# Weight decode without a clamp, scales from column sums, and plain f32 scores for the first eight jobs

## The chip, the core and the metric

The kernel runs on one core of a Trainium2 chip. The metric is the device time of one execution in microseconds. Five engines work beside each other, each taking its own queue of instructions in order: PE (TensorE, matrix products into PSUM), DVE (VectorE), ACT (ScalarE), POOL (GpSimd) and SP, which issues most transfers. Transfers run on 16 DMA engines. Semaphores order the engines; an instruction at the head of a queue that waits holds everything behind it.

## The reference

Attention over 8 batches x 8 heads, 576 positions, 64 numbers a head, then a two-layer network with an odd activation:

```python
scores = scale * np.matmul(q, k.transpose(0, 1, 3, 2))       # scale = 1/8
cum = np.cumsum(np.maximum(s, 0.0), axis=-1)
bias = -(cum[:, :, :, None] - cum[:, :, None, :])
scores = np.where(causal, -1000000000.0, scores + np.minimum(bias, 0.0))
attn = softmax(scores)                                        # sum + 1e-9
x = (attn @ v) as (4608, 512)
h = x @ w_in                                                  # (512, 2048)
g = np.where(h >= 1, h, np.where(h <= -1, 0.0, (h + 1) ** 2 / 4.0))
out = (g @ w_out).astype(np.float32)                          # (2048, 512)
```

q, k, v and s come as float32, the two weights as float64: each weight is read as two 32-bit words.

## The kernel before, in words

**Attention.** A job is a pair of heads and a half of the query positions (320 or 256 of them): 64 jobs, 8 to a batch, jobs 0 to 3 the first halves of batch 0 and jobs 4 to 7 its second halves. `att_load` brings q and k of the job into the raw tiles rq and rk, each twice, into partitions 0 to 63 and 64 to 127. `att_prep` makes from them two pairs of tiles in a reduced f32 form (float32r): Q1 and K1 hold the rounded values (and in the upper half what rounding left of q), Q2 and K2 what rounding left of k, against the rounded q, and four rows more that carry the running sum of s in two parts (`cum`), so that the bias comes out of the same product. It takes three ACT operations (L325, L334, L335), one of DVE (L336) and one of DVE or POOL (L339; POOL for jobs 0 to 11), and two small transfers on ACT's queue for the cum rows. `scores` multiplies Q1 by K1 (L384) and adds Q2 by K2 (L385) in PSUM, six units a job; DVE adds the mask and takes the minimum (L390), ACT the exponent (L401), `weights_t` normalises and splits the weights into two float16 parts (L417 to L428) and a transposing transfer turns them (pt<-pb). `att_out` multiplies with v (L447) and writes the job's piece of the tile x (L458, L459).

**Network.** A half of a batch is one unit. `ffn_h` makes 16 hidden tiles (12 products each, L502), each turned into u by ACT (L514) and DVE (L517, L518) and split into two float16 parts g (L528, L529); `ffn_y` multiplies with the second weight (L541). Three products stand for each product of a float16 pair.

**Weights.** `Weights.decode` turns a tile of 128 x 512 float64 numbers into float32 bits, `scale` finds a power of two from the largest value of a group of tiles, `split` makes the float16 pair. Each weight has 16 tiles. The first weight (w1, tiles wir, held in WO, result WI) is one group; the second (w2, tiles wor, result WO) two groups. In `scale` the maxima of 128 partitions go through PE twice: a transpose (L107) and a product with ones that spreads the result (L117).

**Order.** The program writes the first four jobs with w1's decode in between, then w1's scale and splits, then the loop in which attention runs ahead of the network and w2 is decoded within the first hidden tiles. A scheduler of the language, which works with its own estimate of time and with priorities, then sets the order on each engine's queue. `load(c + 3)` keeps three raw weight tiles ahead of the decode.

## Time and profile before

| | us |
|---|---|
| runs: median, lowest, highest of 3 | 1128.73, 1127.24, 1128.74 |
| profiled execution, span from first to last instruction | 1126.2 |
| profiled execution, own time | not listed apart from its span |
| PE busy | 988.1 (88% of the span) |
| weight loads of PE, beside it | 771.8 (69%) |
| DVE busy | 876.6 (78%) |
| ACT busy | 745.2 (66%) |
| POOL busy | 693.1 (62%) |
| read from HBM, written | 75.33 MB, 9.73 MB |

A row of a group reads: line, engine, operation, out<-in, shapes, count | busy us, mean ns of one | idle us before them and what ended it. A row of the timeline reads: start us, duration us, engine, line. A row of waits reads: who waited for whom: us in total, times, longest. A row by stretches has for PE, its weight loads, DVE, ACT and POOL the busy time and the instructions in brackets, then the clock granted to PE as a share of full speed, the DMA engines' share and their rate in GB/s.

### The profile page before, as it was taken

The page shows a single profiled execution, that of the slowest core. Times are in us where ns is not written, and L with a number is a line of the kernel's source. Part 1 is how long each engine was busy: PE and PEld are TensorE (multiplying, and loading weights), DVE is VectorE, ACT ScalarE, POOL GpSimd, SP SyncE. Part 2 cuts the span into 40 slices and gives each one's busy share as a digit, 9 for nine tenths or more (in the row PEclk, how much of TensorE's full clock was granted, in tenths as well). Part 3 has the DMA queues.
Part 4 walks back from the last instruction along what each step waited for, and adds up shares of the span by engine and source line. Part 5 has one row for each costly group of instructions (what it writes and reads, how often), then busy time and mean ns, then how long its engine had stood idle before and what let it go on. Part 6 is the DMA issues. An engine that isn't in the chain of part 4 may idle for free.

```text
span 1126.2 us, 25201 instructions
## 1 busy us (share of the span) xinstructions
PE 988.1 (88%) x8470; PEld 771.8 (69%) x8470; DVE 876.6 (78%) x2396; ACT 745.2 (66%) x1727; POOL 693.1 (62%) x1177
## 2 busy tenths in 40 slices
PE   1233587799999999989999999999999999899998
PEld 0122355578777877778777877787778777787787
DVE  7999996778777887778778877888788877787533
ACT  4667687677747775767657774777577765777432
POOL 3867279776547764676647754776467664765522
PEclk9997987889999999999999999999999999999999
DMA  8995546677739774778647763877467864666300
GB/s 235 214 204 149 164 110 137 123 158 163 151 74 190 153 172 86 150 170 144 142 86 189 165 143 75 191 169 166 86 148 171 152 136 84 157 156 138 66 24 20
DMA packets 343082, 158.05 MB, mean 140 GB/s; under 512 B 291112, under 2 KB 324264, under 8 KB 342952
## 3 DMA queue, kind: packets, MB, share of 16 engines
q1 hardware_dynamic: 333248, 146.50, 60.7%
q10 hardware_dynamic: 9704, 9.93, 2.8%
q8 instruction: 67, 1.10, 0.4%
q14 instruction: 63, 0.52, 0.1%
HBM read 75.33 MB, written 9.73 MB: 76 GB/s over the span
## 4 chain that ended last, share of the span: by engine, by line
PE 48%; DVE 6%; POOL 5%; issue 3%; ACT 3%; DMA 2%; ACTq 0%; DVEq 0%; POOLq 0%
PE h L502 20%; PE y L541 20%; PE px L447 3%; PE s L384 3%; PE s L385 2%; DMA pt<-pb 2%; DVE pb L428 1%; DVE Q L336 1%; POOL g L529 1%; POOL pb L422 1%; ACT u L514 1%; ACT p L401 1%; POOL vb L350 1%; POOL pb L425 1%; DVE p L390 1%
## 5 line engine op out<-in xcount | busy, mean ns | idle before, releaser
L502 PE MATMUL h<-x,WI 128*128 128x256 f16 (+1 forms) x3072 | 464.7, 291 | 30.3 <-DVE u L518 24.7
L541 PE MATMUL y<-g,WO 128*128 128x256 f16 (+1 forms) x3072 | 456.7, 288 | 7.5 <-POOL g L529 5.3
L502 PEld LDWEIGHTS <-WI 128*128 128x128 f16 x3072 | 291.2, 99 | 124.0 <-issue 34.2
L541 PEld LDWEIGHTS <-WO 128*128 128x128 f16 x3072 | 287.3, 98 | 91.8 <-issue 12.5
L529 POOL TENSOR_TENSOR g<-u,g 128x320 f16<-128x320 f32 (+1 forms) x256 | 204.0, 797 | 162.1 <-ACT g L528 161.3
L401 ACT ACTIVATE p<-p,mn 64x64 f32<-64x64 f32 (+4 forms) x320 | 179.6, 561 | 134.9 <-DVE mn L390 113.1
L514 ACT ACTIVATE u<-h,ub,us 128x320 f32<-128x320 f32 (+1 forms) x256 | 149.3, 584 | 122.8 <-PE h L502 117.8
L517 DVE SCALAR_TENSOR_TENSOR h<-h,ws,u 128x320 f32<-128x320 f32 (+1 forms) x256 | 132.5, 518 | 103.8 <-ACT u L514 101.2
L422 POOL TENSOR_SCALAR pb<-p,rs 64x128 f16<-64x128 f32 (+4 forms) x160 | 97.3, 608 | 165.2 <-DVE rs L418 105.1
L384 PE MATMUL s<-K,Q 128*128 128x288 f32 (+4 forms) x384 | 149.2, 391 | 55.9 <-DVE mn L390 25.9
L425 POOL TENSOR_TENSOR pb<-p,pb 64x128 f16<-64x128 f32 (+4 forms) x160 | 172.8, 1080 | 9.2
L428 DVE SCALAR_TENSOR_TENSOR pb<-p,rs,pb 64x128 f16<-64x128 f32 (+4 forms) x160 | 143.1, 894 | 43.0 <-POOL pb L422 42.7
L390 DVE CUSTOM_DVE_ANT_0 p<-s,mask 64x64 f32<-64x64 f32 (+4 forms) x320 | 134.4, 421 | 27.5 <-PE s L385 24.2
L518 DVE SCALAR_TENSOR_TENSOR u<-u,r,h 128x320 f32<-128x320 f32 (+1 forms) x256 | 130.3, 509 | 6.3
L384 PEld LDWEIGHTS s<-K,Q 128*128 128x128 f32 (+1 forms) x384 | 73.7, 192 | 81.3 <-DVE mn L390 36.1
L385 PE MATMUL s<-K,Q 68*128 68x288 f32 (+4 forms) x384 | 122.3, 320 | 5.1 <-DMA K<-cumd 2.6
L423 ACT ACTIVATE p<-p,rs 64x64 f32<-64x64 f32 (+4 forms) x160 | 89.8, 561 | 55.1 <-DVE rs L418 54.1
L528 ACT CAST g<-u 128x320 f16<-128x320 f32 (+1 forms) x256 | 108.3, 423 | 9.6 <-DVE u L518 9.5
L447 PE MATMUL px<-pt,vt 128*64 128x256 f16 (+3 forms) x1536 | 82.4, 258 | 18.3 <-DMA pt<-pb 8.1
L424 POOL TENSOR_SCALAR pb<-p 64x128 f16<-64x128 f32 (+4 forms) x160 | 91.8, 574 | 10.7 <-ACT p L423 9.5
L447 PEld LDWEIGHTS <-vt 128*64 128x64 f16 x1536 | 73.1, 113 | 36.4 <-issue 28.3
L385 PEld LDWEIGHTS s<-K,Q 68*128 68x128 f32 (+1 forms) x384 | 75.0, 196 | 9.0 <-POOL K L339 3.2
(115 smaller groups left out, 961.4 us busy)
## 6 DMA issues: line engine op xcount, KB each, us to landing
rk<-in_k_dram SPq DMA_DIRECT2D x64, 288.0 KB
rq<-in_q_dram SPq DMA_DIRECT2D x64, 160.0 KB
rk<-in_k_dram SPq DMA_DIRECT2D x64, 160.0 KB
v<-in_v_dram SPq DMA_DIRECT2D x32, 288.0 KB
wir<-in_moe_w_in_dram SPq DMA_DIRECT2D x16, 512.0 KB
rq<-in_q_dram SPq DMA_DIRECT2D x64, 128.0 KB
wor<-in_moe_w_out_dram SPq DMA_DIRECT2D x16, 512.0 KB
out_dram<-o ACTq DMA_DIRECT2D x32, 160.0 KB
```

What stands on the lines that cost most here:

```text
L384: T.matmul(sc[:R, :c1 - c0], Q1[:, hd, qo:qo + R], K1[:, hd, c0:c1], start=True, stop=False)
L385: T.matmul(sc[:R, :c1 - c0], Q2[:KC, hd, qo:qo + R], K2[:KC, hd, c0:c1], start=False, stop=True)
L390: ttr[0] = V.tensor_tensor_reduce(out=Pt[:R, c0:c1], in0=sc[:R, :c1 - c0], in1=mask[:R, mo:mo + c1 - c0], scale=1.0, scalar=3.0e38 if mn i ...
L401: A.activation(Pt[:R, :W], Pt[:R, :W], AF.Exp, bias=m2[:R], scale=-1.0, accum_out=sums[n, i][:R, hd:hd + 1])
L425: G.tensor_tensor(los[1], pw, his[1], ALU.subtract)
L428: V.scalar_tensor_tensor(los[0], pv, rs[:R, :1], his[0], ALU.mult, ALU.subtract)
L447: T.matmul(px[hd * D:(hd + 1) * D, lo:N], VT[:, vl * NB + j, hd * D:(hd + 1) * D], PT[:, 4 * j + 2 * hd + pl, lo:], start=(m == 0), stop=( ...
L502: T.matmul(h[:, :N], WI[4 * kt + ft // 4][:, wl, ft % 4 * P:(ft % 4 + 1) * P], x[:, kt, xl], start=(n == 0), stop=(n == 3 * NKT - 1),)
L514: first = A.activation(u, h[:, :N], AF.Relu, bias=ubi[b], scale=usc[b]).ins
L517: V.scalar_tensor_tensor(h[:, :N], h[:, :N], wsc[b], u, ALU.mult, ALU.max)
L529: G.tensor_tensor(g[:, 1], u, g[:, 0], ALU.subtract)
L541: T.matmul(ys[b, hf, m][:, :N], WO[8 * (m // 2) + ft // 2][:, wl, c0:c0 + P], g[:, gl], start=(ft == 0 and n == 0), stop=(ft == NFT - 1 an ...
```

## The change

**Decode.** ACT copies the high word with a factor 2^-112 in place of taking its magnitude; the clamp with the running maximum (L193) is gone; the shift keeps no mask. A product on PE of ones with the upper 16 bits of every number adds up the columns of each group's tiles in PSUM, and `scale` takes the largest column sum of the group as the bound, which every partition then holds: one reduction of 128 x 512 by DVE and four small operations, with no transpose and no spreading.

**Four scales.** w1's tiles are decoded in another order (all four tiles that a hidden tile needs stand together) and each group of four has a scale of its own, taken as soon as its tiles are decoded. The scales that ACT and DVE apply to the hidden tiles have four columns, one a group; the batch's scale uses the largest of the four.

**First eight jobs.** For jobs 0 to 7 q and k are loaded once, as float32, into one of two pairs of tiles (QF, KF), with the cum rows loaded beside them; there is no preparation. A score is one float32 product over 68 rows, and the mask operation multiplies by -0.125. Jobs from 8 on are prepared as before, with signs turned; Q1 and K1 take the memory of the second pair.

The core of the diff:

```diff
-POOL_LO = {'wi': (2, 3, 7, 11, 15), 'wo': range(16)}
+POOL_LO = {'wi': (8, 12, 13, 14, 15), 'wo': range(16)}
+F32_JOBS = 8
...
+    QF, KF = [], []
+    for i, (tq, tk) in enumerate((("rq", "rk"), ("q1", "k1"))):
+        QF.append(ap.tile([P, 2, NQ], F32, tag=tq, bufs=1, name=f"QF{i}"))
+        KF.append(ap.tile([P, 2, S], F32, tag=tk, bufs=1, name=f"KF{i}"))
+        G.memset(QF[i][D:KC], 8.0)
+        G.memset(KF[i][D:KC], -8.0)
...
-            A.activation(w, hw.bitcast(F32), AF.Abs)
-            V.tensor_scalar(w, w, LEAST_HI, LEAST_HI, ALU.max, ALU.max, accum_out=self.peak[:, c:c + 1])
-            V.tensor_scalar(wi, wi, 3, 0x3FFFFFF8, ALU.logical_shift_left, ALU.bitwise_and)
+            A.activation(w, hw.bitcast(F32), AF.Copy, scale=2.0 ** -112)
+            V.tensor_scalar(wi, wi, 3, None, ALU.logical_shift_left)
+            if n % self.size == 0:
+                self.sums[g] = ps_y.tile([P, 512], F32, tag=f"y{g}", name=f"sum_{self.name}{g}")
+            T.matmul(
+                self.sums[g][:, :NC], ones, w.bitcast(BF16).rearrange("p (n t) -> p n t", t=2)[:, :, 1],
+                start=(n % self.size == 0), stop=(n % self.size == self.size - 1),
+            )
...
         def scale(self, g, least):
-            V.tensor_reduce(t, self.peak[:, g * self.size:(g + 1) * self.size], axis=AX, op=ALU.max)
-            top = column_max(t, f"{self.name}{g}")
-            b = top.bitcast(I32)
-            V.tensor_scalar(b, b, 3, -0x40000000, ALU.logical_shift_left, ALU.bitwise_xor)
-            V.tensor_scalar(b, b, 0x7FFFFFFF, None, ALU.bitwise_and)
-            pow2floor(top, top, least)
-            spread(bound, top, f"{self.name}{g}")
+            V.tensor_reduce(bound, self.sums.pop(g)[:, :NC], axis=AX, op=ALU.max)
+            pow2floor(bound, bound, least)
...
-        WO, WI, ((gp, "g", G_BUFS),), 1,
+        WO, WI, ((gp, "g", G_BUFS),), [n % 4 * 4 + n // 4 for n in range(NW)], 4,
...
     def att_load(n, hf):
...
+        j = jobs.index((n, hf))
+        if j < F32_JOBS:
+            q, k = QF[j % 2], KF[j % 2]
+            for t, src, c0 in ((q[:D, :, :N], qT, q0), (k[:D, :, :W], kT, 0)):
+                LOADQ.dma_start(t, src[b, h0:h0 + 2, :, c0:W].rearrange("h d n -> d h n"))
...
+                CUMQ.dma_start(q[D:D + 2, :, :N], cd[:, :, q0:W])
+                CUMQ.dma_start(k[D + 2:D + 4, :, :W], cd[:, :, :W])
+            return
...
     def att_prep(n, hf):
+        if jobs.index((n, hf)) < F32_JOBS:
+            return
...
+        if j < F32_JOBS:
+            T.matmul(
+                sc[:R, :c1 - c0], QF[j % 2][:KC, hd, qo:qo + R], KF[j % 2][:KC, hd, c0:c1], start=True, stop=True
+            )
+        else:
...
-                scale=1.0, scalar=3.0e38 if mn is None else mn[:R],
+                scale=-0.125 if j < F32_JOBS else -1.0, scalar=3.0e38 if mn is None else mn[:R],
...
                 w1.decode(c)
                 w1.load(c + 3)
+                if k == 6:
+                    w1.scale(j, LEAST_A)
...
-    w1.scale(0, LEAST_A)
+    V.tensor_reduce(a_in, w1.bound, axis=AX, op=ALU.max)
...
     for n in range(NW):
-        c = n % 4 * 4 + n // 4
-        w1.split(c)
+        w1.split(n)
```

How this moves instructions, at three places. On DVE, at the end of w1 (top_wi, t_wi, bound_wi: the scale; pb, rs: attention's weights; x: the piece of the x tile), before:

```order
L428 SCALAR_TENSOR_TENSOR pb_2_747<-p_2_0_729,rs_2_748,pb_2_747 128x3x128
L109 TENSOR_REDUCE top_wi_782<-row_wi_780 1x1
L211 TENSOR_SCALAR top_wi_782<-top_wi_782 1x1
L459 SCALAR_TENSOR_TENSOR x_0_477<-px_0_755,ex_308,x_0_477 128x320
L212 TENSOR_SCALAR top_wi_782<-top_wi_782 1x1
L92 TENSOR_SCALAR top_wi_782<-top_wi_782 1x1
L93 TENSOR_SCALAR top_wi_782<-top_wi_782 1x1
L115 CAST t_wi_788<-top_wi_782 1x1
L118 COPY bound_wi_143<-col_wi_790 128x1
L215 RECIPROCAL r_wi_144<-bound_wi_143 128x1
```

and of the change, the last of its four scales (L199, L214, L215: decode; L219: the reduction; L236: a split):

```order
L214 SCALAR_TENSOR_TENSOR WO_145<-wir_611,WO_145 128x512
L219 TENSOR_REDUCE bound_wi<-sum_wi_607 128x1
L236 SCALAR_TENSOR_TENSOR WI_128<-WO_144,r_wi,WI_128 128x512
L445 TENSOR_SCALAR rs_1_540<-sm_1_520 128x2
L215 SCALAR_TENSOR_TENSOR WO_145<-wir_611,WO_145 128x512
L418 ISA p_2_1_569,mn_2_1_0_573<-s_2_1_0_571,mask 128x320
L418 ISA mn_2_1_0_573 128x1
L90 TENSOR_SCALAR bound_wi<-bound_wi 128x1
L446 RECIPROCAL rs_2_577<-rs_2_577 128x2
```

The scale now stands within the decode of the last tile, in job 2's scores, and splits of earlier groups stand ahead of it; before it stood after job 3's last scores and every split came after it.

On DVE, around the first hidden tiles (h and u of unit 0; L517 and L518 before, L545 and L546 now), before:

```order
L200 SCALAR_TENSOR_TENSOR WO_126<-wor_814,WO_126 128x512
L194 TENSOR_SCALAR WO_127<-WO_127 128x512
L200 SCALAR_TENSOR_TENSOR WO_128<-wor_820,WO_128 128x512
L517 SCALAR_TENSOR_TENSOR h_0_0_902<-h_0_0_902,ws_807,u_0_0_916 128x320
L202 SCALAR_TENSOR_TENSOR WO_127<-wor_817,WO_127 128x512
L517 SCALAR_TENSOR_TENSOR h_0_1_934<-h_0_1_934,ws_807,u_0_1_947 128x320
```

and of the change:

```order
L214 SCALAR_TENSOR_TENSOR WO_139<-wor_909,WO_139 128x512
L219 TENSOR_REDUCE bound_wo<-sum_wo_832 128x1
L215 SCALAR_TENSOR_TENSOR WO_139<-wor_909,WO_139 128x512
L199 TENSOR_SCALAR WO_141<-WO_141 128x512
L90 TENSOR_SCALAR bound_wo<-bound_wo 128x1
L545 SCALAR_TENSOR_TENSOR h_0_0_845<-h_0_0_845,ws_756,u_0_0_859 128x320
L91 TENSOR_SCALAR bound_wo<-bound_wo 128x1
L545 SCALAR_TENSOR_TENSOR h_0_1_877<-h_0_1_877,ws_756,u_0_1_890 128x320
```

Before, the first hidden tile stood among w2's tiles 0 to 2 (WO_126 to WO_128); now eight of w2's sixteen tiles (WO_132 to WO_139) and the first group's reduction stand ahead of it.

On PE, its first rows (s: scores, row_m: the transpose of v's maxima), before:

```order
L384 MATMUL s_0_0_0_211<-K_90,Q_89 64x64
L384 MATMUL s_0_1_0_219<-K_90,Q_89 64x64
L385 MATMUL s_0_0_0_211<-K_92,Q_91 64x64
L385 MATMUL s_0_1_0_219<-K_92,Q_91 64x64
L384 MATMUL s_1_0_0_250<-K_90,Q_89 128x192
L385 MATMUL s_1_0_0_250<-K_92,Q_91 128x192
```

and of the change:

```order
L203 MATMUL sum_wi_185<-WO_134,ones 128x512
L407 MATMUL s_0_0_0_206<-KF_94,QF_93 64x64
L407 MATMUL s_0_1_0_213<-KF_94,QF_93 64x64
L407 MATMUL s_1_0_0_243<-KF_94,QF_93 128x192
L203 LDWEIGHTS ones
L203 MATMUL sum_wi_185<-WO_138,ones 128x512
L407 MATMUL s_1_1_0_254<-KF_94,QF_93 128x192
```

A score is one instruction, and sum products of weight tiles stand between the scores on PE's queue.

More of the change, by code (lines that the diff above doesn't have):

```diff
@@ L64 @@
 W2_RATE = 2
-FIRST_N = 1
 CH_N = 2
@@ L164, in attention_ffn, with __init__, load @@
     class Weights:
-        def __init__(self, name, src, held, out, tags, groups):
-            self.size = NW // groups
+        def __init__(self, name, src, held, out, tags, order, groups):
             self.name, self.src, self.held, self.out, self.tags = name, src, held, out, tags
-            self.peak = cp.tile([P, NW], F32, name=f"peak_{name}")
-            self.bound = [cp.tile([P, 1], F32, name=f"bound_{name}{g}") for g in range(groups)]
-            self.r = [cp.tile([P, 1], F32, name=f"r_{name}{g}") for g in range(groups)]
-            self.raw = {}
+            self.order, self.size = order, NW // groups
+            self.group = {c: n // self.size for n, c in enumerate(order)}
+            self.bound = cp.tile([P, groups], F32, name=f"bound_{name}")
+            self.r = cp.tile([P, groups], F32, name=f"r_{name}")
+            self.raw, self.sums = {}, {}
             self.act_low, self.pool_lo = ACT_LOW[name], POOL_LO[name]
-        def load(self, c, after=None):
-            if c < NW:
-                pool, tag, bufs = self.tags[c % len(self.tags)]
+        def load(self, n, after=None):
+            if n < NW:
+                c = self.order[n]
+                pool, tag, bufs = self.tags[n % len(self.tags)]
                 self.raw[c] = pool.tile([P, NC, 2], I32, tag=tag, bufs=bufs, name=f"{self.name}r{c}")
@@ L184, in load, with decode @@
                 nc.sync.dma_start(dst, src)
-        def decode(self, c):
+        def decode(self, n):
+            c, g = self.order[n], n // self.size
             raw = self.raw.pop(c)
@@ L237, in attention_ffn @@
         .rearrange("(j p) n t -> p j n t", p=P),
-        WO[WO_LAG:], WO, ((ap, "raw", 2), (gp, "x0", 2), (ap, "raw", 2)), 2,
+        WO[WO_LAG:], WO, ((ap, "raw", 2), (gp, "x0", 2), (ap, "raw", 2)), list(range(NW)), 2,
     )
-    a_in, b_out = w1.bound[0], w2.bound
+    a_in = cp.tile([P, 1], F32, name="a_in")
     vraw, csc, rcs, exs, hsc, rsc, usc, wsc, ubi, gsc, ysc, msc = ({} for _ in range(12))
@@ L315, in att_load @@
             for d0 in (0, D):
-                (FIRSTQ if jobs.index((n, hf)) < FIRST_N else LOADQ).dma_start(t[d0:d0 + D], sv)
+                LOADQ.dma_start(t[d0:d0 + D], sv)
         raws[n, hf] = rq, rk
     def att_prep(n, hf):
+        if jobs.index((n, hf)) < F32_JOBS:
+            return
+        if not one:
+            one.append(ap.tile([P, 2, NQ], F32R, tag="q1", bufs=1, name="Q1"))
+            one.append(ap.tile([P, 2, S], F32R, tag="k1", bufs=1, name="K1"))
+        Q1, K1 = one
         rq, rk = raws.pop((n, hf))
@@ L324, in att_prep @@
         cd = cumd[2 * n:2 * n + 2].rearrange("h l n -> l h n")
[L325 to L333 removed]
+        A.activation(Q1[:, :, :N], rq, AF.Copy, scale=0.125)
+        CUMQ.dma_start(Q2[D:D + 2, :, :N].bitcast(F32), cd[:, :, q0:W])
+        CUMQ.dma_start(K2[D + 2:D + 4, :, :W].bitcast(F32), cd[:, :, :W])
         A.copy(K1[:, :, :W], rk)
[L335 removed]
+        A.activation(Q2[:D, :, :N], rq[:D], AF.Copy, scale=0.125)
         V.scalar_tensor_tensor(
[L337 removed]
+            Q1[D:, :, :N], rq[D:], 0.125, Q1[D:, :, :N].bitcast(F32), ALU.mult, ALU.subtract
         )
@@ L383, in scores @@
         sc = ps_s.tile([P, 512], F32, tag="s", name=f"s{n}_{i}_{hd}_{c0}")
-        T.matmul(sc[:R, :c1 - c0], Q1[:, hd, qo:qo + R], K1[:, hd, c0:c1], start=True, stop=False)
-        T.matmul(sc[:R, :c1 - c0], Q2[:KC, hd, qo:qo + R], K2[:KC, hd, c0:c1], start=False, stop=True)
+        j = jobs.index((n, i // 3))
+        if j < F32_JOBS:
+            T.matmul(
+                sc[:R, :c1 - c0], QF[j % 2][:KC, hd, qo:qo + R], KF[j % 2][:KC, hd, c0:c1], start=True, stop=True
+            )
+        else:
+            Q1, K1 = one
+            T.matmul(sc[:R, :c1 - c0], Q1[:, hd, qo:qo + R], K1[:, hd, c0:c1], start=True, stop=False)
+            T.matmul(sc[:R, :c1 - c0], Q2[:KC, hd, qo:qo + R], K2[:KC, hd, c0:c1], start=False, stop=True)
         mn = mins.pop((n, i, hd), None)
@@ L584, in attention_ffn @@
         late.pop(0)()
-    w1.scale(0, LEAST_A)
+    V.tensor_reduce(a_in, w1.bound, axis=AX, op=ALU.max)
     batch_scales(0)
     for c in range(3):
-        w2.load(c, w1.bound[0])
+        w2.load(c, a_in)
     for n in range(NW):
-        c = n % 4 * 4 + n // 4
-        w1.split(c)
+        w1.split(n)
     att_out(*jobs[NPAIR - 1])
```

63 lines of the change are left out of this document (28 added, 35 removed).

## The prediction

> **What bounds the kernel now.** I read the page first for the share of each engine over the whole span, then cut the span into stretches where its rows change character, then asked in each stretch who waits for whom. The page shows PE low in the first sixth and near nine tenths after it:
>
> ```profile
> span 1126.2 us, 25201 instructions
> ...
> PE   1233587799999999989999999999999999899998
> ```
>
> Three events mark the cuts: the last piece of the first x tile is made, the second x tile is complete and its hidden products start in earnest, and the third x tile's products start.
>
> ```profile
> 98.75 0.55 DVE L459 SCALAR_TENSOR_TENSOR x<-px,ex,x 128x320 f16<-128x320 f32 x1 [0.40 <-ACT x L458]
> ...
> 224.34 0.58 PE L502 MATMUL h<-x,WI 128*128 128x256 f16 x2 [0.21 <-ACT x L458]
> ...
> 277.06 1.39 PE L502 MATMUL h<-x,WI 128*128 128x320 f16 x9
> ```
>
> The view by stretches, cut there (PE, weight loads, DVE, ACT, POOL busy us, then clock, DMA share, GB/s):
>
> ```profile
> 0.00:99.00 99.00, 28.10 (x149) 19.37 (x149) 84.77 (x226) 59.84 (x121) 59.84 (x100) 1.00 0.88 216
> 99.00:173.00 74.00, 44.12 (x280) 28.80 (x278) 68.87 (x160) 53.53 (x94) 42.45 (x44) 0.85 0.46 125
> 173.00:225.00 52.00, 40.95 (x294) 28.74 (x293) 35.79 (x97) 36.20 (x75) 44.39 (x58) 0.80 0.66 135
> 225.00:277.00 52.00, 50.90 (x458) 42.45 (x458) 42.12 (x123) 37.96 (x99) 36.45 (x75) 0.92 0.74 158
> 277.00:1045.00 768.00, 747.97 (x6629) 590.12 (x6627) 613.44 (x1727) 528.72 (x1277) 485.07 (x872) 1.00 0.67 142
> ```
>
> From 225 us on PE is busy 97 to 98% of the time: that is matmul-bound, and no instruction before about 200 us matters there except by when it lets PE begin. Before that PE idles. From 0 to 99 us DVE (86%) and the DMA engines (88%) are both nearly full; from 99 to 173 us DVE alone is (93%); from 173 to 225 us no engine is above POOL's 85%. The waits of the first and second stretch say the same: ACT waits for loaded weights, PE for DVE.
>
> ```profile
> ACT WO L192 <- DMA wir<-in_moe_w_in_dram: 16.2, 8, 4.6
> ...
> PE h L502 <- DVE u L518: 24.2, 11, 9.5
> ACT WO L192 <- DMA wor<-in_moe_w_out_dram: 10.6, 7, 2.8
> ```
>
> So I forecast the end as (when the start-up of 225 us is over) plus an unchanged 901 us, and cost each edit by what it takes from DVE and from the transfers in the start-up.
>
> **Part 1, the decode.** The clamp with its running maximum (L193) goes from all 32 weight tiles. Its groups, and its time within the start-up by the stretch view restricted to that line:
>
> ```profile
> L193 DVE TENSOR_SCALAR_CACHE_REDUCE WO<-WO 128x512 f32<-128x512 f32 x32 | 21.5, 676 | 4.7 <-ACT WO L192 4.6
> ...
> 0.00:225.00 225.00, 21.73 (x64) 0.90 0.69 167
> ```
>
> That is 21.7 us of DVE, half (10.9) in each weight. L194 loses its second operation but stays one instruction; alone it already takes 0.41 us where L193, of the same size, takes 0.68, so I cost that at nothing (its row, below, has the least, the median and the longest; the long ones lie beside POOL operations). Abs becomes Copy on ACT: nothing, since ACT is busy 60% and 72% in the two stretches. In exchange DVE reduces six 128x512 sums. The nearest row is a reduction of 576 elements:
>
> ```profile
> L254 DVE TENSOR_REDUCE c<-v 128x1 f32<-128x576 f32 x4 | 3.0, 752 | 0.6 <-DMA v<-in_v_dram 0.6
> ...
> L194 DVE TENSOR_SCALAR WO<-WO x32: 401/414/1433, 8.6 to 158.9; 128x512 int32<-128x512 int32 x32
> ```
>
> Scaled by 512/576 it is 0.67 us: 2.7 us for the first weight's four, 1.3 us for the second's two. The small operations around them are some 20 on both sides: even. The old way from the last maximum to the scale crosses PE twice:
>
> ```profile
> 73.05 0.15 DVE L208 TENSOR_REDUCE t_wi<-peak_wi 128x1 f32<-128x16 f32 x1
> ...
> 85.91 0.27 DVE L109 TENSOR_REDUCE top_wi<-row_wi 1x1 f32<-1x128 f32 x1
> ...
> 88.40 9.91 ACT L221 ACTIVATE WI<-WO,r_wi 128x512 f16<-128x512 f32 x16 [5.17 <-DVE r_wi L216]
> ```
>
> It takes 15 us, but other work fills DVE meanwhile, and the first x tile ends only at 98.75 us; I take no gain for it in the sum, and the order of the change, which splits half of the weight before all of it is loaded, only moves DVE work within the stretch.
>
> The 32 sum products cost PE, by the matmul rows below, 0.21 us for 448 columns at full pace, so 0.24 us for 512: 3.8 us a weight. PE idles 71 us in the first stretch and 41 us from 99 to 225 us; I take zero, and 3.8 us if the second weight's stood on the path.
>
> **Part 2, the first eight jobs.** Gone are three ACT operations, one of DVE and one of POOL a job. DVE's and POOL's, up to 190 us:
>
> ```profile
> L336 DVE SCALAR_TENSOR_TENSOR Q<-rq,Q 64x640 fp32r<-64x640 f32 x4 | 4.7, 1170 | 0.1
> L336 DVE SCALAR_TENSOR_TENSOR Q<-rq,Q 64x512 fp32r<-64x512 f32 x4 | 5.9, 1480 | 0.1
> ...
> L339 POOL TENSOR_TENSOR K<-rk,K 64x1152 fp32r<-64x1152 f32 x4 | 11.4, 2846 | 2.9 <-ACT K L334 2.8
> ...
> 149.14 3.00 DVE L336 SCALAR_TENSOR_TENSOR Q<-rq,Q 64x512 fp32r<-64x512 f32 x1
> ```
>
> 10.6 us of DVE, of which 4.7 for jobs 0 to 3 and 0.7 (job 4, the first of the second form) fall before 99 us and the other 5.2 (3.0 at 149.14 among them) after. Each job's q and k are now loaded once, not twice:
>
> ```profile
> rk<-in_k_dram SPq DMA_DIRECT2D x64, 288.0 KB
> rq<-in_q_dram SPq DMA_DIRECT2D x64, 160.0 KB
> rk<-in_k_dram SPq DMA_DIRECT2D x64, 160.0 KB
> ...
> rq<-in_q_dram SPq DMA_DIRECT2D x64, 128.0 KB
> ```
>
> Before 99 us that saves 4 x (160 + 160) KB and, for jobs 4 and 5, 2 x (128 + 288) KB: 2.16 MB, which at that stretch's 216 GB/s is 10.0 us. SP also issues two DMAs a job fewer. The cum rows are issued on ACT's queue a job earlier; such an issue waits for the job before last to have read the buffer, with ACT's exponents queued behind it, and costs nothing as long as there are two buffers. The second weight's loads (512 KB) come forward on SP's queue, ahead of jobs 5 and 6, into the full first stretch: they take there what they free after it, which I count as even.
>
> The trace has no plain f32 product of this size. Rows of the pair that it replaces, and the only one-instruction f32 product:
>
> ```profile
> L384 PE MATMUL s<-K,Q 128*128 128x288 f32 x12 | 6.1, 509 | 0.1
> L385 PE MATMUL s<-K,Q 68*128 68x288 f32 x12 | 4.5, 375 | 0.0
> L384 PE MATMUL s<-K,Q 128*128 128x448 f32 x7 | 3.5, 529 | 4.5 <-DVE Q L336 2.4 <-DVE mn L390 1.9 <-DVE bound_wo L118 0.3
> L385 PE MATMUL s<-K,Q 68*128 68x448 f32 x6 | 2.5, 449 | 0.0
> L107 PE MATMUL row_m<-ident,mt 128*1 128x128 f32 x1 | 0.4, 373 | 1.4 <-DVE mt L261 1.4
> ...
> 265.13 0.37 PE L384 MATMUL s<-K,Q 128*128 128x448 f32 x1
> 265.34 0.36 PE L385 MATMUL s<-K,Q 68*128 68x448 f32 x1
> ```
>
> Low end: the f32 product costs what L107 suggests, one instruction of the old kind, and the second of each pair is saved: 16 x 0.375 + 8 x 0.449 = 9.6 us of PE for jobs 4 to 7. High end: twice the pair's own time, 16 x 0.88 + 8 x 0.98 = 21.9 us more. I take zero on the path, between them: in 99 to 225 us PE idles 41 us, which hides 21.9; with that cover gone the whole of it counts. Jobs 0 to 3 lie where PE is 28% busy.
>
> The Trainium skill speaks against this edit: its page "FP8 and Floating Point Precision", section TensorE Precision Notes, says that true f32 takes four passes through the array where the reduced form truncates. By it each second-form job (2 x 448 + 4 x 288 = 2048 columns) streams 4096 more, as an estimate 1.9 us at 0.21 us per 448, 7.7 us for four jobs: the sum below stays if PE's idle time hides it and would be 1112 us if none were hidden.
>
> **The sum.** Up to 98.75 us: DVE loses 10.9 + 5.4 - 2.7 = 13.6 us, the transfers 10.0; both are nearly full, so the smaller counts, 10.0. From there to 225 us: DVE loses 10.9 + 5.2 - 1.3 = 14.8 us. Together 24.8 us: the profiled span goes from 1126.2 to 1101.4. No own time is listed for that execution; the runs' median (1128.73) is 2.5 us over its span, so the forecast is 1104 us. What is late next is PE itself.
>
> **Rivals.** A, a smaller gain: the f32 products do stand on the path, because a score's chain (product, masking, exponent) is serial. For it: DVE waits for scores by then.
>
> ```profile
> DVE p L390 <- PE s L385: 8.7, 9, 2.6
> ```
>
> Against it: that is 8.7 of 52 us. Half of the high end, 11 us, gives 1115. B, slower: PE takes its queue in order, and a sum product stands ahead of score products in it, so each wait of a weight tile for its load becomes a wait of attention. The loads' waits are 16.2 + 10.6 us, and each sum also stands behind the shift (32 x 0.41 = 13.1 us): 39.9 us at the most, 1144 us; from 24.8 us (six tenths of it) the change is slower. Against it: PE and ACT wait for those loads today at moments when scores wait too. C, a larger gain: decodes now stand ahead of the first hidden tiles on DVE, the second weight's scale no longer crosses PE, and POOL is rid of 2.8 us a job; then 99 to 225 us shrinks until DVE is as full as in 99 to 173 us (93%): (68.87 + 35.79 - 14.8) / 0.93 = 96.6 for 126 us, 29.4 gained, with the first 10.0: 1089. D: the gain of the start is lost again in the matmul-bound part, or the start-up hangs on the serial chain alone: 1128, no change.
>
> **How the numbers follow.** The forecast (1094 to 1110) has 0.45, A (1110 to 1126) 0.23, C (1078 to 1094) 0.22, B 0.07, D 0.03. The range cuts the outer half-tenths of A and C: 1085 to 1121. A measurement of this kernel tells a change from none at about 0.2%; faster is forecast, A and C, 0.90; same 0.03; slower 0.07.
>
> **What would show it.** Right, if PE reaches its steady rate (the third x tile's products) near 252 us instead of 277, with as many us after it as before, 849. Part 1: DVE busy up to there some 27 us less, six reductions near 0.67 us. Part 2: DMA share of the first stretch lower or the stretch shorter; f32 rows between 0.5 and 1.8 us. It is wrong if the first x tile still ends near 99 us with DVE idle there, if PE's waits on sums exceed 20 us (B), or if the part after the third x tile changes its length.

## The result and the profile after

The changed kernel takes 1112.32 us (median of 4 runs, 1109.51 to 1114.5), the kernel before 1128.74 beside it: 0.9839 of before, 95% interval 0.9816 to 0.9862. It is faster by 16.4 us. The forecast was 1104, with a range of 1085 to 1121. The sign and the range hold; the gain is two thirds of the 24.8 us of the sum, and it falls in the bracket of rival A (1110 to 1126), not in that of the likeliest case (1094 to 1110).

The profiled execution took 1111.73 us, 1.8 us more than its span. Its page, in 40 slices:

```profile
span 1109.9 us, 25082 instructions
...
PE   2456898799999999999999999899999999899998
...
PEclk9955999799999999999999999999999999999999
```

In the first six slices PE has 2, 4, 5, 6, 8 and 9 tenths where it had 1, 2, 3, 3, 5 and 8. The three events of the prediction, from the timeline of the changed kernel (the fourth piece of the first x tile, the last of the second, the first hidden products of the third; L487 and L530 are what L459 and L502 were):

```profile
103.54 0.55 DVE L487 SCALAR_TENSOR_TENSOR x<-px,ex,x 128x320 f16<-128x320 f32 x1
...
204.47 0.47 DVE L487 SCALAR_TENSOR_TENSOR x<-px,ex,x 128x256 f16<-128x256 f32 x1
...
256.25 1.39 PE L530 MATMUL h<-x,WI 128*128 128x320 f16 x9
```

I call the third event the mark. It stands at 256.25 us against 277.06: 20.8 us earlier, where the sum said 24.8 (252). The way there is not the one foretold. The first x tile comes 4.8 us later than before (103.54 against 98.75), where the sum had it 10.0 us earlier; all of the gain is made after it. The views by stretches, cut at these events in each kernel (columns as before), first the kernel before, then the changed one:

```profile
0.00:99.30 99.30, 28.40 (x150) 19.60 (x150) 85.07 (x226) 60.14 (x122) 60.15 (x101) 1.00 0.88 216
99.30:225.30 126.00, 84.85 (x570) 57.33 (x569) 104.66 (x258) 89.44 (x168) 86.85 (x101) 0.83 0.54 129
225.30:277.06 51.76, 50.87 (x457) 42.47 (x457) 41.88 (x123) 38.02 (x99) 36.21 (x75) 0.93 0.75 158
277.06:1126.20 849.14, 823.97 (x7297) 652.42 (x7294) 645.00 (x1794) 557.59 (x1341) 509.90 (x904) 1.00 0.62 132
```

```profile
0.00:104.00 104.00, 46.39 (x164) 22.25 (x166) 83.14 (x214) 59.10 (x118) 64.74 (x106) 0.78 0.80 216
104.00:205.00 101.00, 86.73 (x581) 57.18 (x580) 74.59 (x199) 72.67 (x147) 70.21 (x92) 0.89 0.56 121
205.00:256.25 51.25, 49.17 (x457) 41.41 (x457) 41.51 (x122) 37.89 (x99) 36.46 (x72) 0.97 0.73 158
256.25:1109.90 853.65, 828.53 (x7297) 654.01 (x7294) 647.01 (x1793) 556.17 (x1341) 507.63 (x904) 0.99 0.61 131
```

Three things stand in these rows. DVE has 199.2 us of work up to the mark in place of 231.6: 32.4 us less, somewhat more than the 28.4 us that the sum took off (but not by the sum's terms alone, see the paragraph on the shift below). PE has 182.3 us in place of 164.1, and in the middle stretch the fullest engine is no longer DVE (83%, now 74%) but PE (67%, now 86%). And the last row holds the same 7297 matrix products as before and lasts 853.65 us, 4.5 us longer; this costs the change a fifth of what it won by the mark.

The groups of the changed kernel up to 277 us that answer to L193, L194, L384, L385 and the reductions:

```profile
L407 PE MATMUL s<-KF,QF 68*128 68x288 f32 (+4 forms) x96 | 42.1, 540 | 22.8 <-DVE mn L418 12.0 <-DMA v<-in_v_dram 4.5 <-DVE x L487 3.7
...
L199 DVE TENSOR_SCALAR WO<-WO 128x512 int32<-128x512 int32 x32 | 23.0, 725 | 4.5 <-ACT WO L198 4.3
...
L203 PE MATMUL sum_wi<-WO,ones 128*128 128x512 bf16 x16 | 9.3, 596 | 20.0 <-DVE WO L199 16.6 <-DVE t_m L113 2.4 <-DVE r_wi L222 0.9
...
L203 PE MATMUL sum_wo<-WO,ones 128*128 128x512 bf16 x15 | 8.0, 531 | 6.6 <-DVE WO L199 6.5
...
L219 DVE TENSOR_REDUCE bound_wi<-sum_wi 128x1 f32<-128x512 f32 x4 | 2.7, 672 | 0.0
...
L219 DVE TENSOR_REDUCE bound_wo<-sum_wo 128x1 f32<-128x512 f32 x2 | 1.4, 680 | 0.0
```

Each f32 product is two records, so the 48 products of the eight jobs take 42.1 us (42.3 in e12 below, which was granted the full clock); the 48 pairs that they replace took 23.0 + 18.6 = 41.6:

```profile
0.00:210.00 210.00, 23.01 (x48) 12.05 (x48) 0.92 0.68 167
...
0.00:210.00 210.00, 18.64 (x48) 12.91 (x48) 0.92 0.68 167
```

(the stretch up to 210 us of the kernel before, for L384 and for L385 alone: PE, its weight loads, clock, DMA share, rate). The reductions cost what was foretold, 0.67 us each. The sum products do not: 17.3 us in all (31 of the 32 are in the trace), against 7.7.

### The profile page after: what moved, and what is told of

Its sections match the earlier page's. It is cut to its first block, busy times and chain, and to the rows that moved or that the text cites. A ratio compares the mean times of both kernels' runs of the same rounds, so it can differ in the third digit from the quotient of the medians.

```text
span 1109.9 us, 25082 instructions
## 1 busy us (share of the span) xinstructions
PE 1010.8 (91%) x8495; PEld 774.9 (70%) x8496; DVE 846.3 (76%) x2325; ACT 725.8 (65%) x1703; POOL 679.0 (61%) x1173
## 4 chain that ended last, share of the span: by engine, by line
PE 61%; DVE 12%; POOL 8%; DMA 7%; issue 6%; ACT 5%; ACTq 0%; SPq 0%; DVEq 0%; POOLq 0%
PE y L569 25%; PE h L530 25%; PE px L475 4%; DMA pt<-pb 3%; PE s L412 3%; PE s L413 3%; DVE pb L456 2%; ACT u L542 2%; POOL pb L453 2%; POOL pb L450 2%; DVE p L418 1%; DVE Q L357 1%; DMA vt<-vb 1%; POOL vb L371 1%; DVE h L545 1%
## 5 line engine op out<-in xcount | busy, mean ns | idle before, releaser
L530 PE MATMUL h<-x,WI 128*128 128x256 f16 (+1 forms) x3072 | 463.9, 290 | 7.4 <-ACT x L486 3.4
L530 PEld LDWEIGHTS <-WI 128*128 128x128 f16 x3072 | 291.1, 99 | 97.0 <-issue 13.9
L569 PEld LDWEIGHTS <-WO 128*128 128x128 f16 x3072 | 288.1, 98 | 92.9 <-issue 13.8
L545 DVE SCALAR_TENSOR_TENSOR h<-h,ws,u 128x320 f32<-128x320 f32 (+1 forms) x256 | 132.4, 517 | 110.6 <-ACT u L542 108.1
L456 DVE SCALAR_TENSOR_TENSOR pb<-p,rs,pb 64x128 f16<-64x128 f32 (+4 forms) x160 | 134.6, 841 | 47.1 <-POOL pb L450 47.0
L412 PE MATMUL s<-K,Q 128*64 128x64 f32 (+1 forms) x336 | 126.2, 377 | 16.0 <-DVE mn L418 10.9
L546 DVE SCALAR_TENSOR_TENSOR u<-u,r,h 128x320 f32<-128x320 f32 (+1 forms) x256 | 130.3, 509 | 6.8 <-DVE h L545 0.5
L413 PE MATMUL s<-K,Q 68*64 68x64 f32 (+1 forms) x336 | 102.8, 307 | 2.1 <-DMA K<-cumd 1.3
L452 POOL TENSOR_SCALAR pb<-p 64x128 f16<-64x128 f32 (+4 forms) x160 | 93.2, 583 | 11.9 <-ACT p L451 11.0
L475 PEld LDWEIGHTS <-vt 128*64 128x64 f16 x1536 | 73.4, 113 | 36.7 <-issue 30.2
L412 PEld LDWEIGHTS s<-K,Q 128*64 128x64 f32 (+1 forms) x336 | 61.5, 183 | 27.3 <-DVE mn L418 8.2
L413 PEld LDWEIGHTS s<-K,Q 68*64 68x64 f32 (+1 forms) x336 | 61.9, 184 | 5.8 <-issue 1.7
```

Of the source, the lines that this page charges most:

```text
L412: T.matmul(sc[:R, :c1 - c0], Q1[:, hd, qo:qo + R], K1[:, hd, c0:c1], start=True, stop=False)
L413: T.matmul(sc[:R, :c1 - c0], Q2[:KC, hd, qo:qo + R], K2[:KC, hd, c0:c1], start=False, stop=True)
L456: V.scalar_tensor_tensor(los[0], pv, rs[:R, :1], his[0], ALU.mult, ALU.subtract)
L475: T.matmul(px[hd * D:(hd + 1) * D, lo:N], VT[:, vl * NB + j, hd * D:(hd + 1) * D], PT[:, 4 * j + 2 * hd + pl, lo:], start=(m == 0), stop=( ...
L530: T.matmul(h[:, :N], WI[4 * kt + ft // 4][:, wl, ft % 4 * P:(ft % 4 + 1) * P], x[:, kt, xl], start=(n == 0), stop=(n == 3 * NKT - 1),)
L545: V.scalar_tensor_tensor(h[:, :N], h[:, :N], wsc[b][:, fg:fg + 1], u, ALU.mult, ALU.max)
```

## The experiments

My theory at this point was that of the prediction: the start-up is set by DVE's time and the transfers, both parts relieve them, and PE hides the sums and the f32 products. Twelve runs were made, in three groups of four kernels; each group shared a chip and its own runs of the kernel before, whose median was 1131.58, 1129.2 and 1132.12 us, so ratios are what can be compared. The rest is the time from the mark to the end of the profiled span.

| kernel | mark, us | rest, us | median, us | ratio to before, 95% interval |
|---|---|---|---|---|
| before | 277.06 | 849.1 | 1128.74 | 1 |
| the change | 256.25 | 853.7 | 1112.32 | 0.9839, 0.9816 to 0.9862 |
| e1 decode alone | 269.38 | 859.6 | 1130.66 | 0.9991, 0.9978 to 1.0004 |
| e2 f32 alone | 260.95 | 854.5 | 1112.96 | 0.9840, 0.9808 to 0.9872 |
| e3 f32 products twice | 266.04 | 849.2 | 1120.79 | 0.9915, 0.9897 to 0.9932 |
| e4 sum products twice | 263.86 | 850.7 | 1116.30 | 0.9860, 0.9843 to 0.9877 |
| e5 the change again | 256.53 | 852.0 | 1111.81 | 0.9854, 0.9831 to 0.9877 |
| e6 f32 alone again | 262.03 | 846.6 | 1112.11 | 0.9865, 0.9841 to 0.9889 |
| e7 preparation on the chain | 270.20 | 852.0 | 1123.13 | 0.9950, 0.9933 to 0.9966 |
| e8 preparation off the chain | 262.45 | 856.0 | 1119.64 | 0.9928, 0.9903 to 0.9952 |
| e9 the clamp's time back | 273.25 | 851.9 | 1127.14 | 0.9951, 0.9931 to 0.9970 |
| e10 loads twice | 263.45 | 851.4 | 1118.19 | 0.9875, 0.9861 to 0.9890 |
| e11 GpSimd's part back | 257.17 | 856.7 | 1118.05 | 0.9881, 0.9860 to 0.9902 |
| e12 no splits on GpSimd | 255.72 | 855.6 | 1111.91 | 0.9823, 0.9801 to 0.9844 |

The mark repeats within 1.1 us on another chip (256.25 and 256.53, 260.95 and 262.03); below, marks are compared with the means, 256.4 for the change and 261.5 for f32 alone. The rest does not repeat as well: f32 alone, the same program, had 854.5 and 846.6. All kernels but e1 have 7297 products in it. So small effects of the start-up are read at the mark, and the end is read from the ratios.

**e1, the decode alone.** The kernel before with part 1 only:

```diff
-            A.activation(w, hw.bitcast(F32), AF.Abs)
-            V.tensor_scalar(w, w, LEAST_HI, LEAST_HI, ALU.max, ALU.max, accum_out=self.peak[:, c:c + 1])
-            V.tensor_scalar(wi, wi, 3, 0x3FFFFFF8, ALU.logical_shift_left, ALU.bitwise_and)
+            A.activation(w, hw.bitcast(F32), AF.Copy, scale=2.0 ** -112)
+            V.tensor_scalar(wi, wi, 3, None, ALU.logical_shift_left)
...
+            T.matmul(
+                self.sums[g][:, :NC], ones, w.bitcast(BF16).rearrange("p (n t) -> p n t", t=2)[:, :, 1],
+                start=(n % self.size == 0), stop=(n % self.size == self.size - 1),
+            )
...
```

> The kernel before with the decode change alone (no clamp, sums on TensorE, four scales); the scores of the first eight jobs stay split pairs. By the steps of the prediction: up to 98.75 us DVE loses 10.9 - 2.7 = 8.2 us but the transfers nothing, and both are nearly full, so that stretch gains 0; from there to 225 us DVE loses 10.9 - 1.3 = 9.6. The third x tile's products begin near 267 us and the end is near 1119 us. Rival, DVE alone sets the start-up and the transfers do not: 8.2 + 9.6 = 17.8 us, 1111 us, so that this part alone gives all of the 16.4 us measured. Rival B, the sum products in PE's queue cost what the decode saves: no gain, 1128 us or more.

Measured: 0.9991, no difference that can be told. The first x tile ends at 115.0 us, 15.7 us later than before; the mark comes 7.7 us earlier, but with 23 more products left to do after it, and the rest is 10.5 us longer:

```profile
269.38:1129.00 859.62, 832.62 (x7320) 655.94 (x7318) 656.26 (x1800) 560.27 (x1348) 507.15 (x904) 0.99 0.62 131
```

The mark flatters this kernel: its third unit takes 67.6 us where that of the kernel before takes 62.2, so the fourth begins at 336.96 us against 339.28, only 2.3 us earlier. Both of my numbers fall (1119 and 1111); what is left is the line on rival B. The waits of PE up to 200 us show why it deserves it: PE stands 46.2 us for weight tiles that a sum needs.

```profile
PE sum_wo L197 <- DVE WO L193: 26.5, 8, 10.5
PE s L384 <- DVE mn L390: 20.6, 13, 4.8
PE sum_wi L197 <- DVE WO L193: 19.7, 9, 7.5
```

**e2, the f32 product alone.** The kernel before with part 2 only:

```diff
-        T.matmul(sc[:R, :c1 - c0], Q1[:, hd, qo:qo + R], K1[:, hd, c0:c1], start=True, stop=False)
-        T.matmul(sc[:R, :c1 - c0], Q2[:KC, hd, qo:qo + R], K2[:KC, hd, c0:c1], start=False, stop=True)
+        if j < F32_JOBS:
+            T.matmul(
+                sc[:R, :c1 - c0], QF[j % 2][:KC, hd, qo:qo + R], KF[j % 2][:KC, hd, c0:c1], start=True, stop=True
+            )
...
```

> The kernel before with the plain f32 product for the first eight jobs alone; the clamp and the maxima stay. By the steps of the prediction: up to 98.75 us the smaller of 5.4 us of DVE and 10.0 us of transfers, 5.4, and from there to 225 us 5.2 us of DVE: 10.6, an end near 1118 us. Rival A, the f32 products stand on the serial chain of the scores: in the changed kernel they take 20.6 us of PE after 99 us (14.7 + 5.9) where the pairs that they replace took 15 to 20; half of the first number eats the 10.6: no gain, 1128 us. Rival, with both parts needed together: this part alone gives nothing and so does the other.

Measured: 0.9840, the ratio of the whole change. The mark is 16.1 us earlier than before, where the steps gave 10.6, and the fourth piece of the first x tile comes at 90.2 us, 8.6 earlier. Its four runs spread from 1109.76 to 1117.14 us, and the profiled one is the longest of them. So the second part alone gives all that the end shows, more than I had counted for it, and rival A's reading (no gain) falls.

**e3, every f32 product twice.** The change with

```diff
+            for _ in range(2):
-            T.matmul(
-                sc[:R, :c1 - c0], QF[j % 2][:KC, hd, qo:qo + R], KF[j % 2][:KC, hd, c0:c1], start=True, stop=True
-            )
+                T.matmul(
+                    sc[:R, :c1 - c0], QF[j % 2][:KC, hd, qo:qo + R], KF[j % 2][:KC, hd, c0:c1], start=True, stop=True
+                )
```

> The changed kernel with each plain f32 score product issued twice into the same bank (the second replaces the first). That adds 42.1 us of PE, 21.5 of it up to 99 us and 20.6 after. Theory of the prediction (PE idle hides them): the end moves by less than 3 us from 1112. Rival A (they stand on the chain from a score to its exponent, and PE has little idle time left in the start-up): the third x tile's products come 10 to 25 us later than 256 us, the end is 1122 to 1137 us.

Measured: 0.9915, some 7 to 9 us over the change; the mark 9.6 us later. PE has 27.2 us more, not 42.1, so the second product of each two adds less time than the first:

```profile
L408 PE MATMUL s<-KF,QF 68*128 68x288 f32 (+4 forms) x192 | 69.3, 509 | 13.0 <-DVE mn L419 6.1 <-DMA v<-in_v_dram 4.9 <-DMA KF<-ch 1.9
```

So about a third of the added time stands on the path (9.6 of 27.2), against the less than 3 us of my theory. PE's idle time does not hide everything that is put into it.

**e4, every sum product twice.** The same at the sum product, so that all bounds double:

```diff
+            for i in range(2):
+                T.matmul(
+                    self.sums[g][:, :NC], ones, w.bitcast(BF16).rearrange("p (n t) -> p n t", t=2)[:, :, 1],
+                    start=(n % self.size == 0 and i == 0), stop=(n % self.size == self.size - 1 and i == 1),
+                )
```

> The changed kernel with each sum product issued twice into the same bank, so that all bounds double. That adds 17.3 us of PE, 12.3 up to 99 us and 5.0 after. Theory of the prediction (hidden): less than 2 us from 1112. Rival B (attention's products stand behind them in PE's queue): a third to the whole of 17.3 us, 1118 to 1129 us.

Measured: the mark 7.5 us later for 11.9 us more of PE (29.2 against 17.3); at the end 0.9860, between the two expectations and, with its interval, not told apart from the change (0.9839 and 0.9854). At the mark it speaks against the zero of the prediction: of the time that the sums take of PE about six tenths are not hidden. Part of that may be the clock: up to 104 us this kernel was granted 0.65 of it, the change 0.78.

**e5 and e6, the change and the f32 product alone, beside each other.** Both without a further edit.

> The changed kernel itself, as the control for the three runs beside it on the same chip. 0.984 of the kernel before; the third x tile's products begin at 254 to 258 us; what follows them lasts 849 to 856 us.

> The f32 product alone once more, beside the full change on one chip. If the decode change is worth what its start-up mark says (256.3 against 261.0 us), this kernel is 4 to 5 us slower than the full change, near 0.988 of before. If the decode change is worth nothing, the two agree within 1.5 us.

Measured: 0.9854 and 0.9865, medians 0.3 us apart. The mark of the full change is 5.5 us earlier and its rest 5.4 us longer; since f32 alone had a rest 8 us longer in its other profile, I do not make a cause of that. What the decode change adds to the f32 product at the end is nothing that these runs can tell.

**e7 and e8, the preparation's work put back.** By now I had a new theory: part 2 pays because a serial preparation between load and score is gone. Both kernels put four copies back into each of the first eight jobs of the change, on ACT, DVE and POOL; in e7 q and k themselves go through them, in e8 a scratch tile.

```diff
         if jobs.index((n, hf)) < F32_JOBS:
+            A.copy(q, q)
+            A.copy(k, k)
+            V.tensor_scalar(q, q, 1.0, None, ALU.mult)
+            G.tensor_scalar(k, k, 1.0, 1.0, ALU.mult, ALU.mult)
             return
```

> The changed kernel with four copies in place put between load and product in each of the first eight jobs: q and k on ScalarE, q on VectorE, k on GpSimd, 64 partitions each. About the engine time that the old preparation took, and on the chain from load to score. New theory (the second part pays because the serial preparation between load and score is gone): 6 to 14 us slower than the control. Old theory (VectorE's and the transfers' time): VectorE gets back some 6 to 10 us and the end is 3 to 8 us later, wherever the work stands, so the next run shows the same.

> The same four copies on a scratch tile that nobody waits for (k's copy cut to 880 columns): the engines' time is back, the chain is not. New theory (the chain): within 3 us of the control. Old theory (engine time): as slow as the run with the copies on the chain.

Measured, over the control of the same chip: e7 13.7 us later at the mark and 11.3 us at the end, e8 5.9 and 7.8. So neither theory holds alone. The engines' time and their queues, with no score waiting for the result, bring back 5.9 of the 13.7 us at the mark and 7.8 of the 11.3 at the end; the chain from load to score the rest. The two kernels are not quite alike otherwise: e8 copies 880 columns where e7 copies 1152, and its four copies share one tile, so that POOL stood for DVE's before its own, as this group up to 262 us shows.

```profile
L352 POOL TENSOR_SCALAR dum<-dum 64x640 f32<-64x640 f32 x4 | 4.5, 1130 | 10.2 <-DVE dum L351 10.2
```

**e9, the clamp's time back.** In each of the 32 decodes of the change a maximum with accumulation on a scratch tile:

```diff
+            V.tensor_scalar(dum, dum, 1.0, 1.0, ALU.max, ALU.max, accum_out=peak[:, n:n + 1])
             V.tensor_scalar(wi, wi, 3, None, ALU.logical_shift_left)
```

> The changed kernel with the clamp's time put back on VectorE: in each of the 32 decodes one 128x512 maximum with accumulation on a scratch tile that nobody waits for, 32 x 0.68 = 21.7 us. Theory of the prediction (VectorE's time sets the start-up): all of it counts, 10.9 + 10.9 us less what VectorE idles, 10 to 20 us slower than the changed kernel (1122 to 1132). New theory (removing the clamp brought VectorE little, because the operation beside it grew from 0.52 to 0.74 us, and the end nothing): within 4 us of the changed kernel.

Measured: the mark 16.9 us later, 0.9951 at the end, some 11 to 13 us over the change. My new theory (within 4 us) falls, the prediction's holds: 21.5 us of DVE are worth most of their length at the mark. But f32 alone, which has the clamp itself, ends as early as the change. So what the clamp's removal saves, the other things that the decode change brings spend again. PE's waits up to 200 us name one candidate: the sum products now stand 42.0 us for DVE, in the change 23.1. First e9, then the change:

```profile
PE sum_wi L207 <- DVE WO L203: 28.3, 13, 8.2
PE sum_wo L207 <- DVE WO L203: 13.7, 6, 3.6
```

```profile
PE sum_wi L203 <- DVE WO L199: 16.6, 8, 7.8
PE s L407 <- DVE mn L418: 12.0, 8, 5.5
PE sum_wo L203 <- DVE WO L199: 6.5, 4, 3.0
```

Three kernels make a sum of it at the mark. f32 alone, with the clamp and without sums: 261.5. With the clamp's time and all the rest of the decode change (e9): 273.3, so the rest costs 11.8 us. Without the clamp's time (the change): 256.4, 16.9 less. The decode change is 11.8 spent and 16.9 saved, taken in this order.

PE's busy time up to the mark names another candidate. The rows are f32 alone (e6), e9 and the change:

```profile
0.00:262.03 262.03, 173.13 (x1175) 119.44 (x1176) 214.93 (x596) 170.38 (x364) 168.38 (x270) 0.92 0.67 163
...
0.00:273.25 273.25, 186.73 (x1201) 123.75 (x1202) 213.96 (x596) 170.15 (x363) 167.71 (x271) 0.95 0.67 157
...
0.00:256.25 256.25, 182.29 (x1200) 120.84 (x1202) 199.24 (x533) 169.67 (x363) 171.41 (x270) 0.86 0.69 167
```

PE idles 88.9 us in f32 alone, 86.5 in e9 and 74.0 in the change. With DVE's time equal (214.9 and 214.0 us) PE idles no longer for the sums' waits: they stand where it waited for other things, such as the 19.6 us for u ahead of hidden products in f32 alone, which e9 does not have. What grows from f32 alone to e9 is PE's work, by 13.6 us, and the mark by 11.2. So in this pair the 11.8 us go with the sums as work, more than with their waits.

**e10, the loads twice.** q and k of the first eight jobs come a second time, into partitions that nobody reads:

```diff
+            for t, src, c0 in ((q[KC:, :, :N], qT, q0), (k[KC:, :, :W], kT, 0)):
+                LOADQ.dma_start(t, src[b, h0:h0 + 2, :P - KC, c0:W].rearrange("h d n -> d h n"))
```

> The changed kernel with q and k of the first eight jobs loaded a second time, into partitions 68 to 127 of the same tiles, which nobody reads: the saving in transfers of the second part is undone (4 x 320 and 4 x 416 KB x 60/64, 2.8 MB; two DMAs more a job). Theory of the prediction (the DMA engines nearly full in the first stretch, 10.0 us): 5 to 10 us slower than the changed kernel. Rival (transfers were covered): within 2 us.

Measured: the mark 7.1 us later (263.45), at the end 0.9875, 2 to 4 us over the change. So the saving in transfers counts: with them back the DMA engines are 97% busy up to 99 us where the change has 80%. First e10, then the change:

```profile
0.00:99.00 99.00, 41.85 (x142) 20.20 (x143) 80.53 (x204) 54.46 (x111) 57.80 (x106) 1.00 0.97 230
```

```profile
0.00:99.00 99.00, 42.33 (x143) 20.12 (x144) 81.27 (x211) 56.45 (x115) 64.74 (x106) 0.79 0.80 215
```

**e11, GpSimd's part alone.** Of e8's lines the last alone, on the scratch tile:

```diff
+            G.tensor_scalar(k, k, 1.0, 1.0, ALU.mult, ALU.mult)
```

> The changed kernel with the GpSimd part of the preparation alone put back, one multiplication of 64 partitions x 640 or 880 on a scratch tile in each of the first eight jobs, with nobody waiting: some 10 us of GpSimd. If GpSimd's time sets the pace of the first eight jobs (it makes three of the four operations behind each exponent): 4 to 9 us slower than the changed kernel. If it is ScalarE's or VectorE's time, or the waiting in between: less than 2 us.

Measured: the mark 0.8 us later, so POOL's time does not set the first jobs' pace. At the end 0.9881, 3 to 5 us over the change, all of it in a rest of 856.7 us; by the scatter of the rest I take the mark's word, and leave the end open.

**e12, no splits of the first weight on GpSimd.** This one might also have been a better kernel:

```diff
-POOL_LO = {'wi': (8, 12, 13, 14, 15), 'wo': range(16)}
+POOL_LO = {'wi': (), 'wo': range(16)}
```

> The changed kernel with none of the first weight's splits on GpSimd: five pairs of GpSimd operations (4.4 + 6.2 us) become five of VectorE (4.4 us). If GpSimd sets the pace: 3 to 6 us faster than the changed kernel, 0.980 of before. If VectorE does: 2 to 4 us slower, 0.987.

Measured: 0.9823, the lowest ratio of all, but its interval (0.9801 to 0.9844) holds the change's 0.9839; a better kernel isn't shown. The mark hardly moves (0.7 us). One row does: the shift, which took 23.0 us in the change, takes 17.4 when POOL has no splits of the first weight beside it.

```profile
L199 DVE TENSOR_SCALAR WO<-WO 128x512 int32<-128x512 int32 x32 | 17.4, 546 | 8.5 <-ACT WO L198 8.4
```

Not tried: the decode change without its sums, and without its new order. The 11.8 us above are not divided by a run between the sums, the six reductions (4.1 us of DVE) and the early splits. Nor was part 2 tried with one pair of tiles: in the change a job's loads go into other tiles than those of the job before, and how much of its gain comes from that is open.

## Why the prediction was right, and where it was wrong

**What bounds the kernel: half right.** The start-up was the place; everything won was won before the third x tile. The rest is not the pure matmul bound that I read from 97 to 98%. It varied between 846.6 and 856.7 us with the same 7297 products and PE busy 824 to 830 us, so 22 to 31 us of it are waits. The forecast that it keeps its length was wrong by 4.5 us in this profile. Those 4.5 us are PE's busy time (823.97 and 828.53 us for the same products), not its idle time (25.2 and 25.1), and the clock was granted less: leaving out the last few us, it was half in three stretches of 3.4 us after the mark, and in one before (348.9 us).

```profile
330.80:334.20 3.40, 3.40 (x16) 2.10 (x14) 3.15 (x11) 2.90 (x10) 2.84 (x8) 0.50 1.22 224
576.60:580.00 3.40, 3.25 (x14) 2.03 (x13) 3.25 (x14) 2.63 (x10) 2.53 (x6) 0.50 1.07 217
832.60:836.00 3.40, 3.40 (x19) 2.51 (x17) 1.67 (x6) 1.01 (x4) 2.23 (x5) 0.50 0.97 218
```

Two more stretches of 3.4 us at half clock cost 3.4 us, as an estimate. The changed kernel run again (e5) has one, at 331.1 us, and PE busy 825.3 us, so the other two are not the change's doing; and f32 alone differs by 7.9 us between two profiles.

**Part 1: the step that failed is "PE idles 71 us in the first stretch and 41 us from 99 to 225 us; I take zero".** The sum product was mis-sized: 0.24 us from rows at full pace, 0.56 us measured, 17.3 us in all (the means in e12, at the full clock, are no lower than 0.51 us). And idle time did not hide it: by e4's 7.5 us for 11.9 us of PE, 17.3 us are worth some 11 us at the mark, as an estimate, near the 11.8 of e9. A sum product is also a place in a queue: it waits for its weight tile at the head of PE's queue, and attention's products wait behind it. I had that as rival B, gave it up to 39.9 us and a chance of 0.07, and set 20 us of such waits as the line; the change has 23.1, the decode alone 46.2, and in the runs that delay DVE or the transfers (e8, e10, e7, e9) waits of 28.1, 35.1, 39.6 and 42.0 go with marks 6.1, 7.1, 13.8 and 16.9 us late. That the waits make the delay is argued from this order, and the order does not settle it: each of these edits can bring the weight tiles later by itself, which would lengthen the waits and move the mark alike, and PE's idle time from f32 alone to e9 speaks against it. Nor are the waits all new: the 24.2 us that PE stood before for u (L518) ahead of hidden products are nearly gone in the change, in the same view up to 200 us.

```profile
PE h L530 <- DVE u L546: 2.5, 2, 2.3
```

Rival B was no whole outcome but a debit: the decode change without the clamp's removal costs 11.8 us at the mark, and the removal gives 16.9.

**Part 1: the shift.** "I cost that at nothing" was nearly right at the median (0.41 and 0.43 us) and wrong in the sum: 16.5 us before, 23.0 after.

```profile
L194 DVE TENSOR_SCALAR WO<-WO 128x512 int32<-128x512 int32 x32 | 16.5, 520 | 0.0
```

```profile
L199 DVE TENSOR_SCALAR WO<-WO x32: 397/427/2437, 7.3 to 137.3; 128x512 int32<-128x512 int32 x32
```

All 13 shifts of the change that take over 0.6 us begin while a POOL operation is under way in the timeline, and so do all six before; but so do nine of the change's 19 shorter ones. The Trainium skill, page "SBUF — State Buffer", section "SBUF: two separate sides", says that GpSimd's operations and some forms of VectorE's share one pair of ports as an exclusive lock: whoever starts first keeps it for the whole instruction, and the other waits. The trace agrees in part: the longest shift takes 2.44 us and runs beside POOL's splits and attention's weights, but the nine did not wait. Without POOL's splits of the first weight 5.6 us of the 6.5 are gone (e12); in e9 and e10, which have them, the shifts take 18.1 and 18.7 us, so it matters which operations meet. The clamp itself was never held up:

```profile
L193 DVE TENSOR_SCALAR_CACHE_REDUCE WO<-WO x32: 653/675/687, 7.3 to 156.2; 128x512 f32<-128x512 f32 x32
```

With its time back (e9) the shifts are 4.9 us shorter, which suggests that some of their waits had run out behind the clamp. DVE as a whole lost nothing by it. Up to the mark 21.5 us of clamp and 10.2 of L336 are gone, 4.1 of reductions and 6.5 of shifts came: 21.1 us less, where the rows have 32.4. The other 11 us lie for the most part in operations that the change leaves alone and that ran shorter, such as this one of attention's weights (both up to 277 us, before and in the change):

```profile
L428 DVE SCALAR_TENSOR_TENSOR pb<-p,rs,pb 128x384 f16<-128x384 f32 x8 | 9.5, 1186 | 3.8 <-POOL pb L422 3.8
```

```profile
L456 DVE SCALAR_TENSOR_TENSOR pb<-p,rs,pb 128x384 f16<-128x384 f32 x8 | 6.2, 777 | 0.6 <-POOL pb L450 0.6
```

That DVE's saving came out near the sum's 28.4 us is therefore luck in part.

**The first stretch: 10.0 us foretold, 4.8 lost.** The step "the smaller counts" took the freed time for attention. The second weight took it. Its first operation on DVE starts at 78.58 us, before at 99.38, and seven more shifts start before the first x tile is done (timelines of the kernel before and of the change):

```profile
99.38 0.69 DVE L193 TENSOR_SCALAR_CACHE_REDUCE WO<-WO 128x512 f32<-128x512 f32 x1
```

```profile
78.58 1.00 DVE L199 TENSOR_SCALAR WO<-WO 128x512 int32<-128x512 int32 x1 [0.19 <-ACT WO L198]
```

I had thought of the loads that come forward, "which I count as even", and not of the decodes behind them. That gain was not lost but moved: from the first x tile to the mark the change is 25.6 us shorter, where the sum had 14.8. f32 alone, which leaves this order as it was, has its first x tile 8.6 and 8.8 us earlier than before, 3 us more than its step (5.4).

**Part 2: too small.** Priced alone its steps gave 10.6 us; it gave 16.1 and 15.0 at the mark. The transfers count: e10, which undoes that saving, is 7.1 us late at the mark, where the term had 10.0. What I left out was the chain: ACT's copies, which I priced at nothing, and the waits between them, stood between load and score (e7 against e8: 7.8 us). PE's waits of the kernel before show a part of it, 7.6 us for L336; the 14.5 us for L334 are one wait at the start, and there f32 alone stands 16.7 us for a transfer of the cum rows. The f32 product itself was priced right: zero net, between the two ends, since 48 products take 42.1 us and 48 pairs took 41.6. By the four passes of the Trainium skill (page "FP8 and Floating Point Precision", section TensorE Precision Notes) I had worked out 1112 us if none of them were hidden. The trace agrees with the passes: a product of 448 columns takes 0.92 to 1.02 us once PE is busy. Four times 0.21 and the 0.16 us by which the row of a pair's product (0.37 us) is longer than its pace make 1.00.

```profile
140.50 1.02 PE L407 MATMUL s<-KF,QF 68*128 68x448 f32 x2
...
145.98 0.92 PE L407 MATMUL s<-KF,QF 68*128 68x448 f32 x2
```

That the time came out at 1112 is no proof of that reading: the pairs of the first jobs, on a PE granted 0.80 to 1.00 of its clock, were just as long, and the f32 part alone gives the whole gain.

**The likeliest case and the rivals.** The sum of 24.8 us was 4.0 us too much at the mark and 4.5 us more were lost in the rest. That it came so near at the mark is luck in part: it had 14.2 us from part 1 and 10.6 from part 2, and the marks give 5.1 and 15.6 (means). It also let DVE's 14.8 us count whole up to 225 us, though its own rows have DVE at 69% from 173 us on. Rival A's bracket came, but not by A's mechanism alone: PE's time is on the path by about a third (e3), while the f32 products add only 0.5 us of it. C's condition, a middle stretch that shrinks until DVE is full, did not come: DVE fell to 74% there, and PE became the fullest engine (86%). "What is late next is PE itself" is the sentence that held.

## What to carry to other kernels

Before work is moved from a full engine to one that idles, price it as if a good part of it stood on the path: PE idled 29% of the time up to the mark, and 11.9 us more of sums still came 7.5 us later. Look as well at what the moved work will wait for and at what stands behind it in that queue. Here it made each weight tile a gate for the products behind its sum, and such a gate shows in the waits before it shows in the busy time; the engine's idle time in all then says whether these waits are new or stand in place of others. And where one change has two halves, time each half: here one half alone ended as early as both, and the other spent about what it saved.
